# Adaptive-LayerNorm attention and MLP block with gradients on one Trainium2 core: dO stores by ScalarE, two modulation gradients in the W2 gradient's loop, and another row order in the end stage

## The chip, the cores and the metric

The kernel runs on one core of a Trainium2 chip. The metric is the device time of one execution in microseconds (us); smaller is better. The core's engines have separate instruction streams: TensorE (PE: matmuls and, in a queue of its own, weight loads), VectorE (DVE), ScalarE (ACT), GpSimd (POOL) and SyncE (SP, which here only issues DMAs). DMAs are issued by SP, POOL and, after the change, by ACT. PSUM is the memory that PE writes to; SBUF holds the working tiles.

## What is computed

A block with attention and an MLP, both with LayerNorm and modulation from a condition `c`, forward and backward. With S = 2048 rows, D = 512, 32 heads of 16, F = 1792:

```python
mod = (_silu(c) @ w_mod).reshape(c.shape[0], 6, 1, -1)
sa, ca, ga, sb, cb, gb = (mod[:, 0].copy(), ...)
h = _layernorm(x, axis=-1) * (1 + ca) + sa
x = x + ga * _A_ref(h, A_wqkv, A_wo)
h = _layernorm(x, axis=-1) * (1 + cb) + sb
x = x + gb * _B_ref(h, B_w1, B_b1, B_w2, B_b2)
```

`_A_ref` is softmax attention of 32 heads, then times wo; `_B_ref` is relu(h @ w1 + b1) squared, times w2, plus b2. Beside the block's output (out_0) the kernel returns the gradients of x (out_1), wqkv (out_2), wo (out_3), w1, b1, w2, b2 (out_4 to out_7), c (out_8) and w_mod (out_9), for a given gradient `grad_out` of the output. The gradient of w_mod has six parts of 512 columns, one for each of sa, ca, ga, sb, cb, gb (j = 0 to 5). Part j is the outer product of silu(c) with the summed gradient of that modulation vector; the same sums, multiplied with w_mod, give out_8.

## The kernel before, in words

Rows are cut into 16 tiles of 128 (ST = 16), the rows into four chunks of 512 (SC = 4), D into four blocks of 128 (DT), F into 14 (FT), the heads into eight quads of four (NQ). The run has four stages.

*Forward attention* (about 0 to 985 us): the exponentials of the scores on ACT (L389), the rest on the other engines. While it runs, the MLP and its backward of the chunks that are done run in the background (`gen_mlp`, L1135); it produces dx1, the gradient at the input of the second half, row tile by row tile.

*The middle*, `last_chunk` (about 985 to 1169 us): the last chunk's MLP and its backward, then the weight gradients. `gen_dw1` (L955 to L1015) walks over the 14 blocks of F; each block is 64 matmuls of 128 x 128 into a PSUM tile `dps` (L988, three buffers), one small f32 matmul with a diagonal matrix (L993), four ACT scalings (L1001), and on DVE per block of D a scaling to the output tile dw1 (L1002, two buffers) and two products summed into `dcb_part` and `dsb_part` (L1004, L1007); then POOL stores dw1 to out_4. `gen_dw2` (L1017 to L1061) does the same for w2: 16 matmuls of 128 x 512 a block, two DVE products, an out_6 store on POOL. For both, the first 12 row tiles of the transposed activations come from DRAM through DMA transposes on SP (`turned`: tile tm_blk, four buffers, L941) and the last four row tiles from SBUF (tm_l, one transpose for four blocks, L945, from tile auT for dw1). `turn_do` (L872 to L881) transposes the attention output's gradient dO on PE, copies it by ACT into dOTq and, for every second row tile, stores it to DRAM (L881, on SP). `open_bwd` sets up the tiles of the backward, among them mask tiles `m` that DVE clears (L1344). At its end `last_chunk` issues on SP the loads that the backward starts with, one piece for every eight steps of `gen_dw2`: the operands of the first pair of heads, of the first quad, and WmT, the transposed and modulated wqkv (`load_wmt`, four pieces of 384 KB).

*Backward attention*, `attn_bwd` (about 1166 to 2433 us): for each of eight quads, two pairs of heads; PE, ACT and DVE are each about 98% busy. The gradients ds of the scores are transposed partly by DMA (dsT<-ds, SP). Loads for the next pair are issued by POOL one piece at a time, each behind a small copy (`tick`, L1511) that waits for a point of DVE's work. Pair (7,0) so loads eight pieces.

*The end*, `phase6` (2433 to 2562.6 us): the gradient of wqkv (`dw`, L1572), dx row tile by row tile (`dx`, 12 matmuls of L1664 each, then ACT and DVE, out_1 stores on POOL), the gradient of wo (`dwo`, four blocks of 16 matmuls, L1707, over all 16 row tiles of dx1 in bf16, tile dx1b), and the six parts of the modulation gradient (`mod`: one f32 matmul L1728, an ACT copy L1730, four ACT scalings L1733, one store L1734, four DVE dots L1592). The tile dx1b is cast by ACT (L1702) from the f32 rows of dx1 that `dx` loads (`load_a`, two row tiles at once with three DMA transposes and two loads on SP). `dx` works on a row in place, so the cast stands ahead of ACT's step L1678 on the same tile; the rows 12 to 15 have casts of their own ahead of `dwo(0)`.

Order: PE and SP follow the order in which the program issues everywhere, POOL also from the backward on, and every engine in the end stage, whose order is written out by hand (L1737 to L1813). In the middle the order on DVE, ACT and POOL is the scheduler's. Each engine runs its instructions in order, so an instruction that waits holds all behind it on that engine.

Of the kernel before, what the change touches and what calls it, by code (L numbers as in the profile page):

```python
# [10 lines left out]
F32 = mybir.dt.float32  # L11
# [94 lines left out]
class K:  # L106
# [29 lines left out]
    def build(self, ctx: ExitStack):  # L136
        tc, nc = self.tc, self.nc
        self.dram_pool = ctx.enter_context(tc.tile_pool(name="dram", bufs=1, space=DRAM))
        self.pp = ctx.enter_context(tc.tile_pool(name="persist", bufs=1))
        S, D, F, H, NQ, ST, DT, FT = self.S, self.D, self.F, self.H, self.NQ, self.ST, self.DT, self.FT  # L140
        self.xhat1_d = self.dram("xhat1_d", [S, D], BF16)
        self.qtm_d = self.dram("qtm_d", [NQ, P, ST * 4 * DH], BF16)
        self.ktm_d = self.dram("ktm_d", [NQ, P, ST * 4 * DH], BF16)
        self.QTq_d = self.dram("QTq_d", [NQ, P, S], BF16)
        self.KTq_d = self.dram("KTq_d", [NQ, P, S], BF16)
        self.VTq_d = self.dram("VTq_d", [NQ, P, S], BF16)
        self.dOTq_d = self.dram("dOTq_d", [NQ, P, S], BF16)
        self.O_d = self.dram("O_d", [S, D], BF16)
        self.O32_d = self.dram("O32_d", [S, D], F32)
        self.xhat2_d = self.dram("xhat2_d", [S, D], BF16)  # L150
        self.aT_d = self.dram("aT_d", [FT, P, S], BF16)
        self.duT_d = self.dram("duT_d", [FT, P, S], BF16)
        self.dx1_d = self.dram("dx1_d", [S, D], F32)
        self.vaug_d = self.dram("vaug_d", [P, ST * H * (DH + 1)], BF16)
        self.dOp_d = self.dram("dOp_d", [NQ, P, ST * 4 * DH], BF16)
        self.dqkv_d = self.dram("dqkv_d", [S, 3 * D], BF16)
        self.WmT_d = self.dram("WmT_d", [DT, P, 3 * DT * P], BF16)
        self.open_pools = {}
        self.phase0()
        with tc.manual_schedule(engines={mybir.EngineType.PE, mybir.EngineType.SP}):  # L160
            self.phase_fwd()
            with tc.manual_schedule(engines={mybir.EngineType.PE, mybir.EngineType.SP, mybir.EngineType.Pool}):
                self.phase5()
            with tc.manual_schedule(engines=ALL):
                self.phase6()
        for name in list(self.open_pools)[::-1]:
            self.close_pool(name)
# [98 lines left out]
    def phase_fwd(self):  # L266
# [14 lines left out]
        self.kvs = pp.tile([P, 1], F32, name="kvs")  # L281
        pp.tile([P, 112], BF16, name="pad")
# [474 lines left out]
    def last_chunk(self, bg, O_b, x0s, o32):  # L757
# [116 lines left out]
        def turn_do(k):  # L874
# [4 lines left out]
            if k % 2:  # L879
                t0 = (st0 + k - 1) * P  # L880
                nc.sync.dma_start(self.dOTq_d.rearrange("g p s -> p g s")[:, :, t0:t0 + 2 * P], self.dOTq[:])  # L881
# [44 lines left out]
        pieces = self.pair_pieces(0, 0) + pieces + self.load_wmt()  # L926
# [25 lines left out]
    def gen_dw1(self, sb, xh2, duT):  # L952
# [14 lines left out]
        def load(ft):  # L967
            r = turned(sb, duT, self.duT_d, ft)
# [5 lines left out]
            blks.append((r, w, diag))  # L974

        for ft in range(2):
            load(ft)
        yield 0
        for ft in range(FT):
            if ft + 2 < FT:  # L980
                load(ft + 2)
            else:
                yield ("dw1", 0)
            du, w1_blk, diag = blks[ft]
# [32 lines left out]
    def gen_dw2(self, sb, g_tm, aT, tb):  # L1017
        nc, io = self.nc, self.io
        D, ST, FT = self.D, self.ST, self.FT
# [11 lines left out]

        load(0)
# [3 lines left out]
        for ft in range(FT):  # L1036
# [12 lines left out]
            nc.gpsimd.tensor_tensor(dgb[:], dgb[:], tmp[:], ALU.add)  # L1049
            if ft == FT // 2:  # L1050
# [84 lines left out]
    def gen_mlp(self, sc, O_b):  # L1135
# [63 lines left out]
        for k in range(4):  # L1199
# [11 lines left out]
            nc.vector.tensor_copy(dxb[:], dx1[:])  # L1211
            dxT = mk.tile([P, DT, P], BF16, name="dxT", bufs=2)
# [89 lines left out]
    def phase5(self):  # L1302
# [10 lines left out]
        nc.gpsimd.memset(self.dc_part[:], 0.0)  # L1313
# [34 lines left out]
    def load_wmt(self):  # L1348
# [3 lines left out]
        return [(self.WmT[:, kt].rearrange("p n k -> p (n k)"), self.WmT_d[kt]) for kt in range(DT)]  # L1352
# [37 lines left out]
    def attn_bwd(self):  # L1390
# [97 lines left out]
        for g in range(NQ):  # L1488
            for jp in range(2):
                if jp == 0:  # L1490
                    if g + 1 < NQ:
                        Tn, later = self.load_group(g + 1)
                    else:
                        Tn, later = None, self.wq_pieces(1)
# [103 lines left out]
    def phase6(self):  # L1598
# [44 lines left out]

        def load_a(i):
            s2 = 2 * i
# [12 lines left out]
        def dx(st):  # L1658
            dqT, dx1s = nxt[st // 2]
            k = st % 2  # L1660
# [15 lines left out]
            if st < 12:  # L1676
                cast(st)
# [5 lines left out]
            (nc.sync if st == ST - 1 else nc.gpsimd).dma_start(out1_v[:, st, :], o[:])  # L1683
            if k and st // 2 + 3 < ST // 2:
                load_a(st // 2 + 3)
# [14 lines left out]

        def cast(st):
            nc.scalar.copy(dx1b[:, st, :], nxt[st // 2][1][st % 2][:])  # L1702
# [23 lines left out]
        def mod(j):  # L1726
# [4 lines left out]
            o = sb.tile([P, DT, D], BF16, name="dwm7")  # L1731
            for kt in range(DT):
                nc.scalar.activation(o[:, kt, :], dm[:], ACT.Copy, scale=self.scT[:, kt:kt + 1])  # L1733
            nc.gpsimd.dma_start(dwm_v[:, :, j * D:(j + 1) * D], o[:])  # L1734
# [3 lines left out]
        for j in (5, 3):  # L1738
            load_wmod(j)
        dgs[5] = self.dgb_acc  # L1740
        diag(3, self.dsb_col)
        diag(4, self.dcb_col)
# [8 lines left out]
        dx1b = sb.tile([P, ST, D], BF16, name="dx1b")  # L1751
        O_tm = sb.tile([P, ST, D], BF16, name="O_tm")
# [3 lines left out]
        mod(3)  # L1756
        dx(1)
        load_wmod(4)
        dw(2, 2, dpp, "dp")
        dx(2)  # L1760
        load_wmod(0)
        dw(2, 3, dpp, "dp")
        mod(4)
# [4 lines left out]
        load_wmod(1)  # L1768
# [23 lines left out]
        for st in range(12, ST):  # L1792
            cast(st)
        dwo(0)
        dx(12)
# [90 lines left out]
```

## Time and profile before

| what | value |
|---|---|
| time of four runs | 2564.32, 2573.64, 2564.89, 2577.24 us |
| median | 2569.27 us |
| the profiled execution's own time, and its span | 2564.32 us, 2562.6 us |
| busy in the span: PE, ACT, DVE, POOL | 96%, 90%, 69%, 21% |
| middle, 1075.00 to 1080.00: PE busy | 0.43 of 5.00 us |
| end stage: mean of an ACT cast to dx1b (L1702), and of a scaling for out_9 (L1733) | 608 ns, 711 ns |

The profile is of one execution. Its times are us from the start of the span; a group's row gives the operation with its output and input tiles, the number of instructions, busy time and mean; what stands in brackets behind a row of a timeline is how long the engine had stood idle before it, and whose work ended that idle time. Busy shares are means over stages with different limits: what a change in a stage is worth is read from that stage.

### The profile page before, as it was taken

The numbers are of one execution on the slowest core, as the hardware profiler recorded it, in microseconds if no ns is written. First come the engines' busy times: TensorE is split into PE (matmuls) and PEld (weight loads), VectorE is DVE, ScalarE is ACT, GpSimd is POOL, SyncE is SP. The second block draws the span as 40 slices with busy tenths as digits, with TensorE's granted clock in tenths as the row PEclk, the third lists the DMA queues.
The fourth block names the chain that finished last, engine by engine and source line by source line (L and its number), as shares of the span: only waits on it lengthen the run. The fifth ranks groups of instructions, "written<-read, shape, count | busy, mean of one in ns | idle before, by whom it ended". The sixth has DMA issues, their size and how long they took to land.

```text
span 2562.6 us, 77543 instructions
## 1 busy us (share of the span) xinstructions
PE 2466.9 (96%) x31011; PEld 1225.7 (48%) x31239; DVE 1763.3 (69%) x3651; ACT 2315.4 (90%) x3761; POOL 550.6 (21%) x1098
## 2 busy tenths in 40 slices
PE   8999899999999999999999999999999999999997
PEld 4555555555555554763444444444444444444443
DVE  6222223323322344768999999999999999999876
ACT  7999999999999996417999999999999999999854
POOL 3454521320221121352111111111111111101122
PEclk9999999999999999999999999999999999999998
DMA  4588652440351154799999999999999999999985
GB/s 165 118 183 193 172 95 85 100 112 22 113 127 49 39 135 113 159 208 227 199 199 201 201 200 201 199 204 203 198 203 198 201 204 202 201 198 207 219 218 152
DMA packets 1192481, 424.33 MB, mean 166 GB/s; under 512 B 1137572, under 2 KB 1161254, under 8 KB 1192118
## 3 DMA queue, kind: packets, MB, share of 16 engines
q1 hardware_dynamic: 1156198, 321.87, 65.0%
q0 software_dynamic: 35920, 97.49, 12.7%
q8 instruction: 244, 4.00, 0.7%
q14 instruction: 119, 0.97, 0.1%
HBM read 73.21 MB, written 61.87 MB: 53 GB/s over the span
## 4 chain that ended last, share of the span: by engine, by line
PE 61%; ACT 30%; issue 5%; DMA 3%; DVE 1%; POOL 1%; ACTq 0%; DVEq 0%; POOLq 0%
ACT pu L389 26%; PE st L1523 19%; PE acckv L1416 10%; PE accq L1438 8%; PE st L386 4%; PE dp L1462 2%; ACT pu L1527 2%; PE st L1481 2%; PE dps L1042 2%; PE accbank L320 2%; PE dp L1572 2%; DMA dsT<-ds 1%; PE dps L988 1%; PE st L1664 1%; PE pps L1204 1%
## 5 line engine op out<-in xcount | busy, mean ns | idle before, releaser
L1464 DVE TENSOR_TENSOR ds<-dp,pu 128x512 bf16<-128x512 f32 x2048 | 1236.1, 679 | 13.2 <-PE dp L1462 10.8
L1527 ACT ACTIVATE pu<-st 128x512 bf16<-128x512 f32 x2048 | 1073.9, 612 | 75.5 <-PE st L1523 50.3
L389 ACT ACTIVATE pu<-st 128x1024 bf16<-128x1024 f32 x992 | 912.1, 1077 | 4.9 <-PE st L386 4.3
L386 PE MATMUL st<-QTm,KTq 128*128 128x512 bf16 x1859 | 561.4, 377 | 26.9 <-ACT pu L389 6.0
L320 PEld LDWEIGHTS <-pu 128*128 128x128 bf16 x8192 | 347.3, 96 | 236.1 <-issue 3.1
L320 PE MATMUL accbank<-Vaug,pu 128*128 128x17 bf16 x8192 | 357.6, 171 | 8.3 <-ACT Vaug L520 1.1
L1462 PE MATMUL dp<-m,q 64*128 64x512 bf16 x1024 | 344.4, 381 | 1.1 <-DVE g2w L1048 0.7
L1462 PE MATMUL dp<-m,dOTg 64*128 64x512 bf16 x1024 | 344.0, 381 | 0.0
L1438 PEld LDWEIGHTS <-dsT 128*128 128x128 bf16 x8192 | 239.8, 96 | 214.0 <-issue 208.8
L1523 PE MATMUL st<-m,QTg 64*128 64x512 bf16 x1024 | 319.1, 381 | 9.7 <-ACT pu L1527 8.1
L1523 PE MATMUL st<-m,q 64*128 64x512 bf16 x1024 | 318.8, 381 | 9.5 <-ACT pu L1527 7.3
L386 PEld LDWEIGHTS <-KTq 128*128 128x128 bf16 x1984 | 188.4, 96 | 177.0 <-issue 125.6
L1511 POOL COPY tick<-ds 1x1 bf16<-1x1 bf16 x215 | 37.9, 176 | 1016.2 <-DVE ds L1464 1016.2
L1416 PE MATMUL acckv<-pu,q 128*16 128x512 bf16 x1024 | 154.0, 381 | 0.0
L1416 PE MATMUL acckv<-ds,Qg 128*16 128x512 bf16 x1024 | 154.0, 381 | 0.0
L1416 PE MATMUL acckv<-ds,q 128*16 128x512 bf16 x1024 | 154.0, 381 | 0.0
L1416 PE MATMUL acckv<-pu,dOg 128*16 128x512 bf16 x1024 | 154.0, 381 | 0.0
L1482 ACT COPY dsT<-st 128x512 bf16<-128x512 bf16 x256 | 152.5, 596 | 0.9 <-PE dp L1462 0.4
L1438 PE MATMUL accq<-Kg,dsT 128*128 128x16 bf16 x4096 | 143.5, 170 | 4.2 <-DMA dsT<-ds 4.0
L1438 PE MATMUL accq<-q,dsT 128*128 128x16 bf16 x4096 | 144.0, 170 | 0.4 <-DMA dsT<-ds 0.3
L300 POOL DMA_DIRECT2D QTm<-QTq_d x124 | 63.5, 514 | 341.9 <-PE st L386 320.8
L327 DVE RECIPROCAL rl<-accbank 128x4 f32<-128x4 f32 x128 | 22.9, 179 | 165.2 <-PE accbank L320 164.9
(368 smaller groups left out, 2813.5 us busy)
## 6 DMA issues: line engine op xcount, KB each, us to landing
KTq<-KTq_d POOLq DMA_DIRECT2D x24, 512.0 KB, 4.0
duT_d<-auT POOLq DMA_DIRECT2D x3, 1792.0 KB, 7.7
aT_d<-rT POOLq DMA_DIRECT2D x3, 1792.0 KB, 11.1
KTq_d<-KTq SPq DMA_DIRECT2D x32, 128.0 KB, 1.9
QTq_d<-ev_fm SPq DMA_DIRECT2D x32, 128.0 KB, 3.3
VTq_d<-vT POOLq DMA_DIRECT2D x4, 1024.0 KB, 6.6
dsT<-ds SPq DMA_TRANSPOSE x256, 6.9
dx<-dx_d SPq DMA_DIRECT2D x16, 256.0 KB, 4.0
```

The costliest lines, as they stand in the source:

```text
L300: nc.gpsimd.dma_start(QTm[j][32 * j:32 * j + 32, :], self.QTq_d[g, 32 * j:32 * j + 32, 512 * qc:512 * (qc + 1)])
L320: nc.tensor.matmul(acc[:, a, sub, :], lhsT=pu[:, a, sub * P:(sub + 1) * P], rhs=Vaug[:, kb, h, :], start=(kb == 0 and a == 0 and sub == 0) ...
L386: nc.tensor.matmul(stt[:, a, :], lhsT=KT[:, kb * P:(kb + 1) * P], rhs=QTm[2 * jp + a][:], start=True, stop=True)
L389: nc.scalar.activation(pu[:], stt[:], ACT.Exp, scale=self.scale)
L1042: nc.tensor.matmul(pt[:], lhsT=a[st], rhs=g_tm[:, st, :], start=(st == 0), stop=(st == ST - 1))
L1416: nc.tensor.matmul(acckv[r:r + DH, :], lhsT=T[n][:, ib, col:col + DH], rhs=src[:, a, :], start=(ib == 0), stop=(ib == ST - 1))
L1438: nc.tensor.matmul(accq[:, ib, a, :], lhsT=dsT[:, (i * 2 + a) * 4 + sub, :], rhs=T["K"][:, 4 * c + sub, col:col + DH], start=(c == 0 and i ...
L1462: nc.tensor.matmul(dp[:], lhsT=T["dOT"][rd, ib * P:(ib + 1) * P], rhs=masked["VT"][2 * jp + a][rd, 512 * c:512 * (c + 1)], start=True, sto ...
L1464: nc.vector.tensor_tensor(dsg[:, i, a], dp[:], pu[:, a, :], ALU.mult)
L1482: nc.scalar.copy(dsT[:, 0:4, :], tp[:])
L1523: nc.tensor.matmul(stt[:], lhsT=T["QT"][rs, q], rhs=masked["KT"][2 * jp + a][rs, c0:c0 + 512], start=True, stop=True)
L1527: nc.scalar.activation(pu[:, a, :], stt[:], ACT.Exp, scale=self.scale)
```

## The change

1. *dO stores.* In the last chunk ACT issues the two stores of dOTq to DRAM (L881), right after its copies; SP did.
2. *Blocks three ahead.* `gen_dw1` requests its transposed blocks (tm_blk, tm_l) three blocks ahead, the w1 blocks and diagonals two ahead as they were.
3. *Two modulation gradients* (j = 3, 4: sb and cb) leave the end stage for `gen_dw2`. The diagonal matrices, the w_mod load and eight stores of out_9 (one for each block of D) go with them. Matrices and products lie in the tiles O32 and auT, which are free by then. `dc_part` is cleared at the start of the program.
4. *WmT* is loaded by POOL in eight pieces (196 KB each) in pair (7,0) of the backward, in place of four pieces by SP at the end of the middle.
5. *End stage.* Rows are walked in the order 0 to 7, 12 to 15, 8 to 11. The bf16 rows 8 to 11 of dx1b are written to DRAM (dx1b_d) in the forward, while chunk SC - 2 is worked on, and loaded by one DMA of POOL; the other 12 are cast by ACT inside `dx`, and the four separate casts ahead of `dwo(0)` are gone. The thirteenth dx stands ahead of `dwo(0)`, not behind it. The tile of the out_9 parts (dwm7) is one per block of D with five buffers and a store each, where one tile of four blocks had one buffer and one store. w_mod parts are loaded in the order 5, 0, 1, 2.

```diff
@@ turn_do, last_chunk
-                nc.sync.dma_start(self.dOTq_d.rearrange("g p s -> p g s")[:, :, t0:t0 + 2 * P], self.dOTq[:])
+                nc.scalar.dma_start(self.dOTq_d.rearrange("g p s -> p g s")[:, :, t0:t0 + 2 * P], self.dOTq[:])
...
-        pieces = self.pair_pieces(0, 0) + pieces + self.load_wmt()
+        pieces = self.pair_pieces(0, 0) + pieces
@@ gen_dw1
+        dus = [turned(sb, duT, self.duT_d, ft) for ft in range(3)]
         for ft in range(2):
             load(ft)
         yield 0
         for ft in range(FT):
+            if ft + 3 < FT:
+                dus.append(turned(sb, duT, self.duT_d, ft + 3))
             if ft + 2 < FT:
                 load(ft + 2)
@@ gen_dw2
+        mods = {2: (3, self.dsb_col), 5: (4, self.dcb_col)}
...
+            if ft in mods:
+                j, col = mods[ft]
+                if ft == min(mods):
+                    low = self.ra.tile([P, FT * 512], BF16, name="auT")
+                    hi = self.ra.tile([P, 4, D], F32, name="O32")
+                    nw = DT * D
...
+                nc.gpsimd.dma_start(wm, io["w_mod"].rearrange("(kt p) n -> p kt n", p=P)[:, :, j * D:(j + 1) * D])
+                for kt in range(DT):
+                    nc.scalar.activation(dg[:, kt * P:(kt + 1) * P], self.ident_f[:], ACT.Copy, scale=col[:, kt:kt + 1])
+            if ft - 2 in mods:
+                pt = self.dps.tile([P, 512], F32, name="dps")
+                nc.tensor.matmul(pt[:], lhsT=self.ones_f[:], rhs=dg, start=True, stop=True)
+                yield 2
+                nc.scalar.copy(dm, pt[:])
+                for kt in range(DT):
+                    c = 2 * nw + kt * D
+                    o = low[:, c:c + D]
+                    nc.scalar.activation(o, dm, ACT.Copy, scale=self.scT[:, kt:kt + 1])
+                    nc.gpsimd.dma_start(io["out_9"][kt * P:(kt + 1) * P, j * D:(j + 1) * D], o)
+                    c = 2 * nw + DT * D
+                    nc.vector.scalar_tensor_tensor(low[:, c:c + D], dm, 1.0, wm[:, kt], ALU.mult, ALU.mult,
+                                                   accum_out=self.dc_part[:, kt, j:j + 1])
@@ gen_mlp
+            if sc == SC - 2:
+                nc.gpsimd.dma_start(self.dx1b_d.rearrange("(st p) d -> p st d", p=P)[:, k, :], dxb[:])
@@ load_wmt
-        return [(self.WmT[:, kt].rearrange("p n k -> p (n k)"), self.WmT_d[kt]) for kt in range(DT)]
+        return [(self.WmT[:, kt, n:n + 6].rearrange("p n k -> p (n k)"), self.WmT_d[kt, :, n * P:(n + 6) * P])
+                for kt in range(DT) for n in range(0, 3 * DT, 6)]
@@ attn_bwd
-                        Tn, later = None, self.wq_pieces(1)
+                        Tn, later = None, self.wq_pieces(1) + self.load_wmt()
@@ phase6
+        order = [*range(ST - 8), *range(ST - 4, ST), *range(ST - 8, ST - 4)]
...
-            if st < 12:
-                cast(st)
+            if n < ST - 4:
+                nc.scalar.copy(dx1b[:, st, :], gp[:])
...
-            o = sb.tile([P, DT, D], BF16, name="dwm7")
             for kt in range(DT):
-                nc.scalar.activation(o[:, kt, :], dm[:], ACT.Copy, scale=self.scT[:, kt:kt + 1])
-            nc.gpsimd.dma_start(dwm_v[:, :, j * D:(j + 1) * D], o[:])
+                o = sb.tile([P, D], BF16, name="dwm7", bufs=5)
+                nc.scalar.activation(o[:], dm[:], ACT.Copy, scale=self.scT[:, kt:kt + 1])
+                nc.gpsimd.dma_start(dwm_v[:, kt, j * D:(j + 1) * D], o[:])
...
-        for j in (5, 3):
+        for j in (5, 0):
             load_wmod(j)
         dgs[5] = self.dgb_acc
-        diag(3, self.dsb_col)
-        diag(4, self.dcb_col)
...
+        nc.gpsimd.dma_start(dx1b[:, ST - 8:ST - 4, :], tm_v(self.dx1b_d))
...
-        mod(3)
         dx(1)
-        load_wmod(4)
+        load_wmod(1)
...
-        load_wmod(0)
         dw(2, 3, dpp, "dp")
-        mod(4)
         dx(3)
...
-        load_wmod(1)
...
         dx(11)
-        for st in range(12, ST):
-            cast(st)
+        dx(12)
         dwo(0)
-        dx(12)
```

## The prediction, made before the changed kernel ran

> **What bounds the kernel now.** I read the engines' busy shares first, then the chain of work that ended last, then the stretches of the two stages that the change touches. TensorE (PE) is busy for 2466.9 of 2562.6 us, and the chain says the same of the path:
>
> ```profile
> PE 2466.9 (96%) x31011; PEld 1225.7 (48%) x31239; DVE 1763.3 (69%) x3651; ACT 2315.4 (90%) x3761; POOL 550.6 (21%) x1098
> PE 61%; ACT 30%; issue 5%; DMA 3%; DVE 1%; POOL 1%; ACTq 0%; DVEq 0%; POOLq 0%
> ```
>
> ACT's 30% are the exponentials of forward attention (L389), which the change doesn't touch. So I look only for time in which PE stands still, or runs slowly, in the middle (about 990 to 1169 us) and in the end stage (2433 to 2562.6). The middle's busy time by stretches (columns: window, its length, busy PE, PEld, DVE, ACT, POOL, granted clock, DMA share, GB/s) and PE's timeline:
>
> ```profile
> 1070.00:1075.00 5.00, 5.00 (x91) 4.99 (x88) 3.50 (x15) 1.80 (x6) 2.44 (x4) 1.00 1.39 212
> 1075.00:1080.00 5.00, 0.43 (x5) 0.26 (x3) 3.48 (x14) 0.00 (x0) 1.19 (x2) 0.93 1.05 200
> 1080.00:1085.00 5.00, 4.80 (x46) 4.80 (x46) 3.99 (x18) 1.80 (x6) 0.75 (x1) 0.50 0.59 130
> ```
> ```profile
> 1080.19 1.44 PE L988 MATMUL dps<-tm_blk,xh 128*128 128x128 bf16 x12 [4.76 <-DVE junk L1004]
> ```
>
> PE stands 4.76 us for a PSUM buffer of dps that VectorE (DVE) must free, and then works at clock 0.50 and 0.89: the 64 matmuls of that block take 6.55 us instead of 3.57, so 3 us more, and 0.46 us of waiting follows at 1091.3. In all 8.2 us. Why DVE was late stands in its timeline:
>
> ```profile
> 1068.89 0.91 DVE L1344 MEMSET m<- 128x1024 uint32 x1 [2.22 <-DMA dOTq_d<-dOTq]
> ...
> 1076.19 0.35 DVE L1002 SCALAR_TENSOR_TENSOR dw<-dps,opcbT,t 128x128 bf16<-128x128 f32 x1 [2.38 <-DMA out_dram<-dw]
> ```
>
> The memset of a mask tile waits until the second dO store has landed; behind it stand the steps of dw1, whose store then goes out late (1070.52) and makes the block two later wait. The store of dO is SP's:
>
> ```profile
> 1050.62 0.37 SPq L881 DMA_DIRECT2D dOTq_d<-dOTq  x1
> 1051.04 7.15 SPq L941 DMA_TRANSPOSE tm_blk<-duT_d  x3
> ...
> 1062.90 0.37 SPq L881 DMA_DIRECT2D dOTq_d<-dOTq  x1
> ```
>
> In the end stage PE is continuous from 2433.65 to 2507.6 and is held before and within the first block of dwo (L1707), by ACT:
>
> ```profile
> 2518.25 2.32 PE L1707 MATMUL gps<-dx1b,O_tm 128*128 128x512 bf16 x9
> 2523.89 0.59 PE L1707 MATMUL gps<-dx1b,O_tm 128*128 128x512 bf16 x1 [3.32 <-ACT dx1b L1702]
> 2526.14 0.58 PE L1707 MATMUL gps<-dx1b,O_tm 128*128 128x512 bf16 x1 [1.66 <-ACT dx1b L1702]
> 2528.01 2.14 PE L1707 MATMUL gps<-dx1b,O_tm 128*128 128x512 bf16 x4 [1.28 <-DMA out_dram<-dx]
> ```
> ```profile
> 2520.20 2.56 ACT L1733 ACTIVATE dwm<-dm,scT 128x512 bf16<-128x512 f32 x4 [2.26 <-DMA out_dram<-dwm]
> ...
> 2527.35 2.16 ACT L1702 CAST dx1b<-dx 128x512 bf16<-128x512 f32 x4
> ```
>
> ACT waits 2.26 us for the store of the one dwm buffer; the casts of rows 10 and 11 come late after it, and four more (rows 12 to 15) follow. PE's last four matmuls of the block and the 12 of dx(12) then take 2.14 and 4.26 us, where a later four take 1.03 and a later 12 take 2.59: slow clock after the gap.
>
> [...]clock 0.50 after the 4.76 us gap, back within 6.6 us; after 3.32 + 1.66 us, a block at half speed. [...] The trace of before has no store from ACT here; it shows that the second store, issued after SP's run of transposes, needed 5.99 us (1062.90 to 1068.89).
>
> **The change, part by part**, against the profiled execution (2564.32 us: span 2562.6 and 1.7 around it, 4.95 under the median of 2569.27; I take the difference over to the median).
>
> *End stage, dwo.* From 2518.25 to the end of dwo(3) at 2547.35 PE needs 29.10 us. Its work there is 64 dwo matmuls (16 take 3.45 in the chain: 13.80) and two dx of 12 (2.59 each: 5.18), 18.98 in all. In the new order dx(12) goes ahead of dwo(0), rows 8 to 11 of dx1b come by DMA from a copy made in the forward, dwm has five buffers so that the 2.26 us wait goes, and the four casts of 2.16 us go (12 of 16 casts stay, each with its dx). Moving ACT's steps forward by 2.26, the cast of the last row wanted ends at about 2524.05; PE does dx(12) from 2518.25 to 2520.84 and reaches the last matmul of dwo(0) near 2524.1. What is late next is this cast, by 0.1 to 0.5. So 29.10 - 18.98 - 0.1 = **-10.0 us**. The transposes for dx(12), which SP issues up to 2511.9 and which need 5.1 to 5.8 us to land, and the 0.5 MB load on POOL far ahead, are covered by 2518.25.
>
> *End stage, two modulation gradients less.* Each is a f32 matmul of 0.86 us on PE, in a stretch where PE never stops: **-1.72**. Their ACT work (8 diagonals, 2.5 us; twice 0.57 + 4 x 0.64), 8 DVE dots of 0.77 (6.2), two loads and two stores on POOL ran beside PE: 0.
>
> *The same two in the middle.* PE is continuous from 1086 to 1166 as well: **+1.72**. DVE's 6.2 us: it is busy 8.6 to 8.9 of 10 us in dw1 but, by its blocks, about 13 of 25 us in dw2: 0. ACT is at 4.7 of 10: 0. POOL gets two loads (0.76 each) and eight stores (0.54), at 5.5 of 10: 0 by time. By order not: the first load goes into the old auT and waits until the last tm_l, issued by SP at 1096.59 with a landing of 3.7 to 7.9, has read it (1100.3 to 1104.5). Behind it on POOL stand the dw1 stores of blocks 8 and on and later w1 loads; DVE waits for those stores, PE for DVE. The slack of dps at blocks 11 to 13 is 2.1 us, then 1.1 to 2.9 in dw2. Bounds 0 to +2.5; I take **+0.8**.
>
> *dO stores on ACT, blocks three ahead.* SP loses two issues, ACT gains two (0.37 each, PE doesn't wait for ACT here). ACT's copy for the second store ends at 1062.87 and SP issued at 1062.90: no earlier issue. The transposes of blocks 2 and 3 leave at about 1027, where the DMA share is 0.91 falling to 0.26, and not at 1051; tm_blk has four buffers, so "three ahead" takes SP no further than the buffers did. So the store may land earlier by 0 to 2.5 us (4.1 to 4.5 is the median landing of such stores). Against it: DVE's order moves. The first memset stands three operations sooner, two stand ahead of block 2's last step (its store goes out 1.7 us later after the landing), and six, not five, ahead of block 3's last (+0.91). One fewer is left behind it, so the 0.46 wait goes. The 4.76 us stall becomes 3.3 to 6.3: bounds -8.2 (also the clock loss goes) to +1.5; I take **-0.5**.
>
> *WmT in eight pieces on POOL during pair (7,0), not by SP at 1162.* PE waits 1.0 us for dsT in 1260 to 2420, and a pair with 16 pieces on POOL (2340 to 2420) has PE busy 78.70 of 80 against 78.80 with eight. 0; if the 1.57 MB held the dsT transposes back for their own length at 200 GB/s, +7.9. At the handover PE waits 1.0 us: 0 to -1.0. *Forward*: four 128 KB stores more on POOL and a memset at the start, neither near PE's waits: 0 (0 to +0.5).
>
> Sum: -10.0 - 1.72 + 1.72 + 0.8 - 0.5 = **-9.7 us**: 2554.6 for the profiled execution, 2559.6 on the median.
>
> **The rivals.**
> A, *the stall in the middle goes too* (0.25): with the early transposes the dO store lands in 4 us[...]. For it: DMA share 1.10 to 1.39 at 1060 to 1075, by traffic that moves away. Against: DVE's new order. A further -7.7: 2551.9.
> B, *the end gains only part* (0.17): dx(12) or the last casts are late for another reason (transposes land after 2518, ACT still behind with mod(1)). Then only the wait of 2.26 and 1.72 go, with +2 in the middle: 2567.3. Against it: the transposes have 6 us.
> C, *POOL held by the w_mod load* (0.08): if tm_l lands much later than 7.9 us, the dw1 stores stop, dw has two buffers, DVE stops two blocks later (7.7 us of PE time), PE after dps's slack of 2.1. Up to a hold of about 10 us nothing much is lost; each us more costs one[...]. It decides from a hold of about 20 us, where the loss passes 10 and eats the end's gain. At 25 us: 15 + 3 - 11.7 + 1.7, so +8: 2577. Against it: no landing over 7.9 for tm_l.
> That the stores' move does nothing (the change not doing what it says there) is inside my forecast.
>
> **How the numbers follow.** Forecast 0.50 (its own range 2554 to 2564), A 0.25, B 0.17, C 0.08. The range 2549 to 2570 takes in A and B with 1 in 10 left out at either end. A measurement of this kernel can tell 0.5%, 12.8 us: under 2556.4 is faster. Faster: 0.22 of A, 0.10 of the forecast: 0.32. Slower, over 2582: 0.04, of C and of what I didn't see. Same: 0.64.
>
> **What would show it.** Right: dwo(0) to dwo(3) with dx(12), dx(13) in about 19.1 us of PE with no wait over 0.5; mods at about 1115 to 1145 with no new PE wait; a wait for junk L1004's successor near 1075 of 3.3 to 6.3 us, with clock 0.50 after it. A is right if that clock stays 1.00; B if PE still waits over 2 us for ACT or dqT near 2518 to 2528; C if PE waits for dps at 1100 to 1125. Wrong altogether if pair (7,0) shows PE waits for dsT over 1 us, or the end has a wait elsewhere (the dg wait of 1.03 at 2507.6 growing).

## The result and the profile after

The changed kernel takes 2560.35 us (median of 37 runs, 2555.39 to 2570.23), the kernel before 2566.20 in the runs beside it (58 runs, 2561.02 to 2588.31). The ratio is 0.9972, with a 95% interval of 0.9961 to 0.9982: about 7.2 us less, where 9.7 had been forecast. The medians differ by 5.85 us. The gain is clear of noise, but smaller than the 12.8 us at which the forecast would have called the kernel faster. The profiled execution took 2560.64 us, its span is 2558.8; it is 3.7 us shorter than the profiled one of before. From the page of the changed kernel, the busy time of each engine and the chain's shares by engine:

```profile
PE 2465.3 (96%) x31011; PEld 1223.4 (48%) x31239; DVE 1766.6 (69%) x3651; ACT 2314.8 (90%) x3757; POOL 567.9 (22%) x1137
PE 60%; ACT 30%; issue 5%; DMA 3%; DVE 1%; POOL 1%; DVEq 0%; ACTq 0%; POOLq 0%
```

PE is as full as before, so a comparison of stages has to tell it. I cut each execution at four marks that both traces have: the small f32 matmul that closes the first block of dw1 (block 0), the first score matmul of the backward, the first matmul `dp<-dk_t` at its end, and the end of the span.

| stage | before | after | difference |
|---|---|---|---|
| start to the small matmul of dw1's block 0 | 1055.36 | 1055.29 | -0.07 |
| middle, from there to the backward | 110.96 | 117.54 | +6.58 |
| backward | 1259.83 | 1262.91 | +3.08 |
| end | 136.45 | 123.06 | -13.39 |

So the end stage gave more than was forecast for it (11.7), and the middle took more than was forecast for it (2.0). The middle first. Its 6.58 us have three parts: the first ten blocks of dw1, with the stall at 1075, take 42.82 us for 43.39 (-0.57); from there to the first matmul of the W2 gradient on tm_l it takes 23.70 us for 18.27 (+5.43, all of it new loss); the rest is longer by the two matmuls of the modulation gradients (+1.72). PE's timeline after the change, around 1080 (start, duration, operation, idle time before it and who ended it), and the stretches of the middle (columns as in the prediction):

```profile
1080.81 1.44 PE L992 MATMUL dps<-tm_blk,xh 128*128 128x128 bf16 x12 [4.48 <-DVE junk L1008]
```

```profile
1075.00:1080.00 5.00, 1.33 (x21) 1.16 (x19) 3.07 (x15) 0.43 (x2) 0.77 (x3) 1.00 1.25 200
1080.00:1085.00 5.00, 4.20 (x51) 4.19 (x51) 4.64 (x21) 1.80 (x6) 1.16 (x2) 0.66 0.20 62
...
1110.00:1122.00 12.00, 8.41 (x79) 5.53 (x79) 8.54 (x56) 3.60 (x12) 3.60 (x5) 0.86 1.12 190
```

Before the change the last of these stretches was:

```profile
1110.00:1122.00 12.00, 11.95 (x112) 7.85 (x111) 9.99 (x59) 3.60 (x12) 3.79 (x6) 1.00 1.06 204
```

The stall at 1075 is still there: 0.80, 4.48 and 0.65 us of waits and a block of 4.93 us in place of 3.57, 7.29 us against 8.20 before. The waits themselves are longer than before (5.93 us for 5.22). What is shorter is the slow clock: by the record of the granted clock that each trace has, it lasted 3.41 us here (1080.30 to 1083.71) and 6.83 us before (1079.31 to 1086.14). The memset still waits for the dO store, which takes as long when ACT issues it (issued 1062.83, landed 1068.56: 5.73 us) as when SP did (5.99). DVE's timeline after the change:

```profile
1068.56 0.91 DVE L1375 MEMSET m<- 128x1024 uint32 x1 [2.80 <-DMA dOTq_d<-dOTq]
...
1108.34 0.35 DVE L1006 SCALAR_TENSOR_TENSOR dw<-dps,opcbT,t 128x128 bf16<-128x128 f32 x1 [2.56 <-DMA out_dram<-dw]
...
1114.52 0.35 DVE L1006 SCALAR_TENSOR_TENSOR dw<-dps,opcbT,t 128x128 bf16<-128x128 f32 x1 [2.87 <-DMA out_dram<-dw]
```

The last two are new: blocks 10 and 11 of dw1 wait for the stores of blocks 8 and 9. POOL's timeline shows why, and PE's what it cost:

```profile
1102.65 0.76 POOL L1064 DMA_DIRECT2D auT<-in_w_mod_dram  x1 [3.10 <-DMA tm_l<-auT]
1103.40 0.76 POOL L1014 DMA_DIRECT2D out_dram<-dw  x1
...
1105.31 0.80 POOL L1064 DMA_DIRECT2D auT<-in_w_mod_dram  x1
1106.10 0.76 POOL L1014 DMA_DIRECT2D out_dram<-dw  x1
```

```profile
1111.36 0.83 PE L992 MATMUL dps<-tm_blk,xh 128*128 128x128 bf16 x12 [1.27 <-DVE junk L1008]
...
1117.54 0.38 PE L1047 MATMUL dps<-g_tm,tm_blk 128*128 128x512 bf16 x1 [2.16 <-DVE junk L1008]
1118.07 3.90 PE L1047 MATMUL dps<-g_tm,tm_blk 128*128 128x512 bf16 x10 [0.16 <-issue]
```

And the same matmuls of the W2 gradient in the kernel before, then the stretch of those ten matmuls after the change, with a granted clock of 0.59:

```profile
1114.43 2.75 PE L1042 MATMUL dps<-g_tm,tm_blk 128*128 128x512 bf16 x11
```

```profile
1118.07:1121.97 3.90, 3.90 (x11) 1.50 (x11) 3.56 (x24) 1.64 (x6) 0.71 (x1) 0.59 1.17 230
```

The scheduler put both w_mod loads between the dw1 stores. The first waits 3.10 us for the last tm_l. The store behind it goes out at 1103.40 and block 10 may start only at 1108.34; the store of block 9 follows at 1106.10, right behind a second load of 512 KB, and block 11 starts at 1114.52, 8.4 us later (the median landing of these stores was 4.1 before). PE waits 3.43 us in two parts. Ten matmuls then take 3.90 us at a mean granted clock of 0.59, where eleven took 2.75 in the kernel before (a few records of matmuls are missing in a trace, here one of the block's twelve in either; from the first of them to the first on tm_l it is 4.27 us for 2.59).

In the end stage the chain of the changed kernel, in pieces (start, duration, engine and line) goes through dx and dwo without a gap:

```profile
2519.70 7.77 PE st L1699 x36
...
2527.53 6.89 PE gps L1739 x31
2534.42 2.59 PE st L1699 x12
...
2543.92 2.60 PE st L1699 x12
```

36 matmuls of dx(10), dx(11) and dx(12) are followed at once by dwo(0). From the start of dx(12), 2527.53 - 2.59 = 2524.94, to the end of dwo(3) at 2543.92 it is 18.98 us, where it was 29.10. That makes -10.1 of the stage's 13.39 us. Another 1.7 us lie at its very start, up to the column sums (10.78 us for 12.46), where PE waits for the last dsT, before and after:

```profile
2431.64 0.92 PE L1438 MATMUL accq<-Kg,dsT 128*128 128x16 bf16 x28 [3.29 <-DMA dsT<-ds]
```

```profile
2440.57 0.86 PE L1470 MATMUL accq<-Kg,dsT 128*128 128x16 bf16 x28 [2.62 <-DMA dsT<-ds]
```

This part isn't the change's: over all traces it takes 8.3 to 14.9 us.

### The profile page after: what moved, and what is told of

It is laid out like the page before. It is cut to its first block, busy times and chain, and to the rows that moved or that the text cites. A ratio compares the mean times of both kernels' runs of the same rounds, so it can differ in the third digit from the quotient of the medians.

```text
span 2558.8 us, 77624 instructions
## 1 busy us (share of the span) xinstructions
PE 2465.3 (96%) x31011; PEld 1223.4 (48%) x31239; DVE 1766.6 (69%) x3651; ACT 2314.8 (90%) x3757; POOL 567.9 (22%) x1137
## 4 chain that ended last, share of the span: by engine, by line
PE 60%; ACT 30%; issue 5%; DMA 3%; DVE 1%; POOL 1%; DVEq 0%; ACTq 0%; POOLq 0%
ACT pu L391 26%; PE st L1555 19%; PE acckv L1448 10%; PE accq L1470 8%; PE st L388 4%; PE dp L1494 3%; ACT pu L1559 2%; PE st L1513 2%; PE dps L1047 2%; DMA dsT<-ds 2%; PE accbank L322 2%; PE dp L1604 1%; PE st L1699 1%; PE pps L1234 1%; PE dps L992 1%
## 5 line engine op out<-in xcount | busy, mean ns | idle before, releaser
L1496 DVE TENSOR_TENSOR ds<-dp,pu 128x512 bf16<-128x512 f32 x2048 | 1236.4, 679 | 15.8 <-PE dp L1494 12.8
```

The source lines that it names most:

```text
L1496: nc.vector.tensor_tensor(dsg[:, i, a], dp[:], pu[:, a, :], ALU.mult)
```

## The experiments

All are edits of the changed kernel, or put parts of it on the kernel before; each is compared with runs of the kernel before on the same chip. The stages are cut as above; they are of one profiled execution each, and that isn't always a typical one: those of e1, f1 and i4 were the longest of their kernel, that of g1 lay 13.7 us above its median.

| run | ratio to before, interval | middle | backward | end | PE's waits for dqT |
|---|---|---|---|---|---|
| after | 0.9972, 0.9961 to 0.9982 | 117.54 | 1262.91 | 123.06 | 0 |
| e1_mods_in_end | 0.9954, 0.9935 to 0.9972 | 111.68 | 1263.23 | 135.05 | 0 |
| e3_wmt_by_sp | 0.9975, 0.9962 to 0.9989 | 118.24 | 1261.40 | 122.60 | 0 |
| f1_wmod_by_sp | 0.9958, 0.9941 to 0.9975 | 113.22 | 1261.30 | 131.11 | 6.7 |
| f2_masks_by_act | 0.9927, 0.9907 to 0.9947 | 106.68 | 1263.14 | 122.27 | 0 |
| g1_masks_wmod_wmt | 0.9919, 0.9895 to 0.9944 | 104.60 | 1262.01 | 139.42 | 13.5 |
| h1_end_stage_alone | 0.9991, 0.9969 to 1.0014 | 110.79 | 1264.52 | 142.17 | 13.2 |
| h2_one_dwm_buffer | 0.9981, 0.9964 to 0.9998 | 115.50 | 1263.09 | 135.73 | 8.0 |
| h3_stores_sp_two_ahead | 0.9948, 0.9934 to 0.9963 | 117.11 | 1262.14 | 128.20 | 3.9 |
| i4_masks_wmod | 0.9897, 0.9861 to 0.9933 | 104.33 | 1259.53 | 135.12 | 8.1 |
| k2_end_alone_no_O | 0.9974, 0.9959 to 0.9989 | 109.82 | 1263.75 | 130.33 | 0 |
| h4_row_order_as_before | 0.9973, 0.9957 to 0.9989 | 119.30 | 1262.98 | 128.35 | 0 |
| k4_masks_mods_in_end | 0.9899, 0.9865 to 0.9932 | 102.61 | 1262.21 | 123.34 | 0 |

The runs e1 to f2 shared one chip, g1 to h3 a second one, i4 to k4 a third, so ratios of different groups are compared with care. How much one stage differs between executions shows in the middle of the five kernels that have the two w_mod loads on POOL and the memsets on DVE (after, e3, h2, h3, h4): 115.50 to 119.30 us.

**e1_mods_in_end**: the block in `gen_dw2` goes, the calls in the end stage come back.

```diff
-            if ft in mods:
-                ...
+        diag(3, self.dsb_col)
+        diag(4, self.dcb_col)
...
+        mod(3)
         dx(1)
+        load_wmod(4)
...
+        mod(4)
         dx(3)
```

> The changed kernel with the two modulation gradients (j = 3, 4) back in the end stage; all else as changed. Theory (the w_mod load on POOL, with the dw1 stores behind it, cost the middle 5.1 us beyond the 1.72 us of PE work): the PE waits of 1.27 and 2.16 us at 1110 to 1118 and the slow clock after them are gone, the backward starts at about 1166.0 in place of 1172.8, the end stage is 1.7 to 2 us longer, so 4.5 to 5 us less in all (about 2555.5 on the median of 2560.4). Rival (the dO stores and DVE's order of memsets cause the late waits): the backward still starts after 1170 and the time is the same within 1.5 us.

The backward starts at 1165.72, as the theory says, and the two late waits are gone: the middle is 5.86 us shorter. The rival's cause, DVE's order, is ruled out for the late waits. The time is 0.9954 of before; its interval overlaps that of the changed kernel, so the gain is shown in the trace and not in the time. (The profiled execution was the longest of this kernel, with ACT 5.55 us behind an out_9 store in the end stage.)

**e3_wmt_by_sp**: WmT by SP at the end of the middle, four pieces.

```diff
-                        Tn, later = None, self.wq_pieces(1) + self.load_wmt()
+                        Tn, later = None, self.wq_pieces(1)
...
-        pieces = self.pair_pieces(0, 0) + pieces
+        pieces = self.pair_pieces(0, 0) + pieces + self.load_wmt()
```

> The changed kernel with WmT loaded by SP in four pieces at the end of the middle, as before. Theory (WmT's pieces on POOL push the dsT transposes back in pair (7,0)): the PE waits for dsT of 1.30 and 0.81 us at 2329 and 2340 are gone and the backward, from its first matmul to the first dp<-dk_t, takes about 2 us less than 1262.9; the time falls by 1 to 2 us. Rival (the longer backward is what differs from one execution to the next anyway): 1262 to 1264, with waits for dsT of 2 us or more elsewhere, and the time the same within 1 us.

The two waits in pair (7,0) are gone, as the theory says, but the time isn't shorter: the ratio is that of the changed kernel. In their place PE waits at the start of the backward, for ACT's copy to dsT. First the changed kernel's longer wait in pair (7,0), then this one:

```profile
2329.51 0.46 PE L1470 MATMUL accq<-Kg,dsT 128*128 128x16 bf16 x12 [1.30 <-DMA dsT<-ds]
```

```profile
1178.21 0.58 PE L1554 MATMUL st<-m,q 64*128 64x512 bf16 x1 [1.59 <-ACT dsT L1513]
```

All traces together say the same. With WmT on POOL, five of nine have a wait of 1.30 to 1.75 us for dsT at this place of pair (7,0); with WmT on SP, none of five. With WmT on SP all five wait 0.30 to 2.25 us for ACT's copy at the start; with WmT on POOL, none of nine. So WmT's place seems to move a wait, from the start of the backward to pair (7,0). Over all traces the backward takes 1259.5 to 1263.2 us with WmT on POOL (nine executions, mean 1262.3) and 1259.8 to 1264.5 with WmT on SP (five, mean 1262.3): the 3.08 us of the first table are what one execution differs from another. In the middle this execution had the stall of 1075 at 7.56 us, because the store of block 2 landed later still (DVE waited 4.69); its late waits were 0.83. Which store lands late varies; a wait of PE of 4.3 us or more near 1080 stands in all ten traces with the memsets on DVE.

**f1_wmod_by_sp**: one word.

```diff
-                nc.gpsimd.dma_start(wm, io["w_mod"]...
+                nc.sync.dma_start(wm, io["w_mod"]...
```

> The changed kernel with the two w_mod loads of the W2 gradient's loop issued by SP, between its transposes, in place of POOL. Theory (POOL's order: the load waits for auT with the dw1 stores behind it, and its 0.5 MB go ahead of theirs): the waits of 1.27 and 2.16 us are gone, the backward starts at about 1168.0, 4.8 us less. Rival (the 1 MB and eight stores more are the load, whoever issues them): PE still waits 3 us or more between 1108 and 1160, and the time is the same within 1.5 us.

The backward starts at 1168.39, 4.4 us earlier; PE has no wait for dps after 1092. The same bytes, issued between SP's transposes, cost nothing there:

```profile
1123.91 0.95 SPq L1064 DMA_DIRECT2D auT<-in_w_mod_dram  x1
```

So it was not the traffic as such. The edit changes two things, though: the engine that issues, and the time, as SP gets to the loads about 20 and 30 us later than POOL did. Whether POOL's wait of 3.10 us, the bytes that POOL issues ahead of the stores, or the traffic at just that time cost most isn't separated.

**f2_masks_by_act**: ACT writes the zeros of the mask tiles, from dcb_col times 0, so that they can't be scheduled before dw1 is done.

```diff
-        for ms in self.masked.values():
-            for m in ms:
-                nc.vector.memset(m, 0.0)
...
         fill.until("half")
+        for ms in self.masked.values():
+            for m in ms:
+                nc.scalar.activation(m, self.dcb_col[:, 0:1].to_broadcast([P, self.S]), ACT.Copy, scale=0.0)
```

> The changed kernel with the eight mask tiles cleared by ACT once dcb_col is there (at about 1120), in place of DVE's memsets, which wait for the dO store. Theory (the memset that waits for the dO store, and the memsets, make DVE late and so PE): the waits of 0.80, 4.48 and 0.65 us and the slow block near 1072 to 1091 are gone, the backward starts at about 1165.5, 7.3 us less, if ACT's 15 us of clearing fit beside the W2 gradient. Rival (dw1 has two buffers and its stores need 5 us to land, so DVE is held by them without any memset): PE still waits over 2 us for dps between 1065 and 1095, and the gain is under 3 us.

All waits before 1095 are gone, and one of 2.20 us is left at 1113.6 with no slow clock after it (12 matmuls in 2.75 us). The middle is 10.9 us shorter than in the changed kernel, more than the 7.3 expected: 7.8 us come from the first ten blocks of dw1, and the rest because the loss by the late stores fell from 5.4 to 2.4 us. That DVE, 7.3 us of memsets lighter (8 x 0.91), meets those stores with more slack is a likely reason, not a shown one. The edit takes from DVE both the wait for the store and the memsets' own time; which of the two counts more isn't separated. ACT's clearing took 14.6 us (12.68 for seven tiles and 1.91) beside the W2 gradient. The waits of PE between 1040 and 1165, in all:

```profile
PE dps L1050 <- DVE junk L1011: 2.2, 1, 2.2
PE dp L1494 <- DVE g2w L1056: 0.7, 1, 0.7
PE dp L1494 <- DVE ds L1496: 0.3, 1, 0.3
```

**g1_masks_wmod_wmt**: f1, f2 and e3 together.

> The changed kernel with all three moves: masks cleared by ACT, w_mod loads of the W2 gradient by SP, WmT by SP at the end of the middle. Theory (three separate costs): the backward starts at about 1158.0, that is 2.2 us before the 1160.3 of the version with the masks alone, its last wait for dps (2.20) being gone, and the backward is 1 to 2 us shorter: about 2544.5 on the median, against 2548.0. Rival (the middle is then bound by something else, DMA or POOL, and SP's queue before the backward by WmT): no gain over 2548.0.

The middle is as expected: the backward starts at 1158.27 and no wait for dps is left. The time doesn't decide: the medians are 2547.82 and 2548.02 us, but from two chips, on which the kernel before differs by 5 us (2569.15 and 2564.09), and the intervals of the two ratios (0.9919 and 0.9927) overlap. The profiled execution took 2561.5 us and lost 13.5 us in the end stage, to which nothing had been done. PE's timeline there:

```profile
2515.43 7.33 PE L1698 MATMUL st<-WmT,dqT 128*128 128x512 bf16 x24 [9.44 <-DMA dqT<-dq_t]
```

SP's, in the same execution: one transpose sat 12.04 us in SP's queue, where the median of these eight was 2.75.

```profile
2491.92 12.04 SPq L1681 DMA_TRANSPOSE dqT<-dv_t  x1
```

**h1_end_stage_alone**: the kernel before with part 5 of the change only (w_mod parts loaded in the order of before).

> The kernel before with the end stage of the change alone (row order, rows 8 to 11 of dx1b by DMA with their stores in the forward, dwm in five buffers, dx(12) ahead of dwo(0)); the modulation gradients, the dO stores, the blocks and WmT as before. Theory (the prediction's step): dwo(0) to dwo(3) with dx(12) and dx(13) take 19 to 20 us of PE in place of 29.1, the time falls by 9 to 10.5 us. Rival (with the two modulation gradients still in the end stage ACT is late anyway, and the gain needs both): 3 to 6 us.

Neither: 0.9991, its runs spread from 2557.49 to 2578.18. There is no wait for ACT's casts, and the first dwo matmul to the last take 16.6 us, as in the changed kernel (16.4; 29.1 before, with dx(12) among them). So the part does what was meant, but ahead of it PE waits 13.2 us for dqT (9.8 at once):

```profile
PE st L1670 <- DMA dqT<-dq_t: 13.2, 3, 9.8
```

```profile
2450.00:2530.00 80.00, 67.36 (x298) 29.18 (x297) 54.70 (x143) 39.87 (x81) 27.57 (x47) 0.94 1.15 213
```

The second fence is the stretch 2450 to 2530 of the same trace: DMA share 1.15.

**k2_end_alone_no_O**: h1, and the 2 MB of O_tm left out.

```diff
-            nc.gpsimd.dma_start(O_tm[:, b, :], tm_v(self.O_d)[:, b, :])
+            nc.gpsimd.memset(O_tm[:, b, :], 0.0)
```

> The end stage of the change alone on the kernel before, as in the earlier run with a ratio of 0.9991, but with the four loads of O_tm (2 MB) in the end stage left out: POOL clears the tile, so out_3 and what is made of it are zero. Theory (the DMA engines are full in the end stage, and the dqT transposes come late because of it): the waits for dqT fall from 13 us to under 3, ratio 0.993 to 0.996. Rival (ACT is late with six modulation gradients in the end stage, or the chip was just slow): dqT waits as before or waits for ACT of 5 us or more, ratio over 0.998.

The waits for dqT are gone, the DMA share of the stretch is 0.88, and PE is busy for 78.97 of 80 us:

```profile
2450.00:2530.00 80.00, 78.97 (x405) 35.30 (x398) 61.11 (x159) 48.55 (x97) 33.42 (x51) 1.00 0.88 225
```

The median is 2562.91 us (before on this chip 2569.01), where h1 had 2571.72 (before 2569.15). The ratio, 0.9974, is less good than the theory's 0.993 to 0.996, and its interval overlaps that of h1. So the crowded DMA engines as the cause of the waits are supported by one trace on each side, no more: two kernels with the same end stage, g1 and the changed one, show 13.5 and 0 us. How much of the time these waits take on average isn't settled. A rival that wasn't tried alone is the change's own load of 0.5 MB into dx1b: the two traces without it (before, h4) have no wait for dqT, six of the twelve with it have one.

**h2_one_dwm_buffer**: one tile and one store for a part again.

```diff
             for kt in range(DT):
-                o = sb.tile([P, D], BF16, name="dwm7", bufs=5)
-                nc.scalar.activation(o[:], dm[:], ACT.Copy, scale=self.scT[:, kt:kt + 1])
-                nc.gpsimd.dma_start(dwm_v[:, kt, j * D:(j + 1) * D], o[:])
+                nc.scalar.activation(o[:, kt, :], dm[:], ACT.Copy, scale=self.scT[:, kt:kt + 1])
+            nc.gpsimd.dma_start(dwm_v[:, :, j * D:(j + 1) * D], o[:])
```

> The changed kernel with one dwm tile of four blocks and one store again. Theory (the 2.26 us wait for the store is the first cause of the late casts): ACT waits 2 to 3 us before the second part, PE 1.5 to 4 us near the end of dwo(0)[...], so 2 to 6 us more. Rival (dx(12) ahead of dwo(0) hides it): less than 1 us more.

ACT waits 6.42 us for the store (0.16 in the changed kernel), but PE only 0.2 for ACT, as it had just waited 6.43 for dqT. The ratio is 0.9981. The wait on ACT is as the theory says; whether it reaches PE when dqT is on time stays open.

**h3_stores_sp_two_ahead**: `nc.sync` in place of `nc.scalar` for the dO stores, and `turned` back in `load`, two blocks ahead.

> The changed kernel with the dO stores issued by SP and the blocks two ahead again. Theory (these parts don't set the stall at 1075 to 1086, DVE's memset behind the store and the memsets do, and the store's data are ready at the same time): the backward starts within 1.5 us of 1172.8, the waits before 1095 keep a sum of 5 to 7 us, the time is the same within 1.5 us. Rival[...]: the backward starts 2 us or more later.

The middle takes 117.11 us, 0.4 less than with these parts, with waits of 5.01 and 3.40 us: the theory holds, parts 1 and 2 don't shorten the middle. All traces bear it out. Where nothing is lost (f2, g1, i4, k4) the first ten blocks of dw1 take 35.04 us; with the old stores and two blocks ahead (before, h1, k2, h3) they take 42.25 to 43.39, with the new ones (after, e1, e3, f1, h2, h4) 42.82 to 47.81. The ratio, 0.9948, is better than that of the changed kernel, 6 us for which these blocks are too little; the two were not timed on one chip, and I leave it open.

**h4_row_order_as_before**: rows 0 to 15, four casts, dx(12) behind dwo(0), no bf16 rows through DRAM; dwm keeps its five buffers.

```diff
-        order = [*range(ST - 8), *range(ST - 4, ST), *range(ST - 8, ST - 4)]
+        order = [*range(ST)]
...
-        dx(12)
+        for st in range(12, ST):
+            nc.scalar.copy(dx1b[:, st, :], nxt[st // 2][1][st % 2][:])
         dwo(0)
+        dx(12)
```

> The changed kernel with rows 0 to 15 in order, four separate casts ahead of dwo(0), dx(12) behind it, and no bf16 copy through DRAM; dwm stays at five buffers. Theory (the order and the casts carry most of the 10 us, the buffers 2 to 3): PE waits 3 to 5 us for dx1b casts in dwo(0), with slow clock after it, 5 to 8 us more than the changed kernel, ratio to before 0.999 to 1.001. Rival (the end stage is bound by its DMAs, so the order hardly matters, and 0.5 MB less is loaded): within 2 us of the changed kernel, ratio 0.996 to 0.998.

In the trace the theory holds: PE waits 1.02, 2.00 and 1.28 us for casts, four matmuls then take 2.15 us, and the end stage is 5.3 us longer than after. Its dwo matmuls take 26.5 us from the first to the last, where before they took 29.1 and in the twelve traces with the new order 16.4 to 17.8, without dx(12)'s 2.6. So the order and the casts carry most of the step, the five buffers about 2.6. The ratio, 0.9973, is in the rival's range. Both can be true if in the runs that don't wait for casts dqT is late at the same place; that isn't shown.

**i4_masks_wmod**: f1 and f2 together.

> The changed kernel with the masks cleared by ACT and the two w_mod loads by SP; WmT by POOL as changed. Theory (memsets on DVE and the w_mod load on POOL are the whole loss of the middle): no wait for dps, backward starts at 1158.3 within 0.3, no wait for dsT copies at its start; ratio to before 0.990 to 0.993. Rival (the end stage is bound by its DMAs and takes back what comes earlier): ratio 0.994 or more, with waits for dqT that grow by what the middle gave.

**k4_masks_mods_in_end**: e1 and f2 together.

> The changed kernel with the masks cleared by ACT and the two modulation gradients back in the end stage. Theory (their move takes 2 MB of DMA and 1.72 us of PE out of a crowded end stage and costs the middle about 4 us by POOL's order): the backward starts at about 1156.5, dqT waits in the end stage are larger than with the gradients moved, and the time is 0 to 4 us over that of the version with masks by ACT and w_mod by SP. Rival (moving them never pays): 2 us or more below that version.

i4 starts its backward at 1158.25, without any wait for dps: the memsets and the place of the w_mod loads were the whole avoidable loss of the middle, 117.54 - 104.33 = 13.2 us (the two matmuls stay). k4 starts it at 1157.75; its middle is 102.61 us, 1.72 less than that of i4, just the two matmuls of 0.86. In the time the two can't be told apart: the ratios are 0.9897 and 0.9899, each with an interval of 9 us to either side, and k4's median is 2.15 us the higher one. So whether moving the two gradients pays, once their loads don't stand on POOL, stays open. That they relieve the end stage's DMA isn't shown: the profiled execution of k4 had no wait for dqT, that of i4, the longest of six, 8.1 us. Both beat the kernel before and the changed one; i4's median is 2544.23 us, beside 2569.01 before.

## Why the prediction was right, and where its steps were off

The likeliest case was right in direction and in its main step; the measured gain is about 7.2 us for 9.7 forecast. That the sum came so near is in part luck. In the two traces the middle lost 4.6 us more than forecast and the backward 3.1, the end stage gave 1.7 more, and the medians differ by more than these two executions. And the forecast of 2559.6 us lies so close to 2560.35 because it started from a median of four runs, 2569.27, where 58 runs give 2566.20.

- *dwo*: -10.0 forecast; 29.10 became 18.98 in the trace, -10.1. Right, and not by chance: the step is as short in every trace with the new order. What was late next, the last cast, didn't show. As time of the whole kernel it isn't shown alone: h1 has the short step and a ratio of 0.9991, h4 the longer one and that of the changed kernel.
- *Two gradients out of the end, into the middle*: -1.72 and +1.72. In the middle i4 against k4 gives 1.72. In the end stage, from the column sums (2438.61 before, 2446.52 after) to the start of dx(12), it is 79.64 against 78.42 us, 1.2 less, in one execution each.
- *dO stores and blocks*: -0.5 forecast, 8.20 became 7.29, -0.9. The number is luck. Right is that the memset and the store stayed in each other's way and that the clock fell to 0.50; only f2 removed that. But the waits grew by 0.71 us, the 0.46 us wait that I said would go became 0.65, and the gain is a slow clock of 3.41 us in place of 6.83. In f1 and h4, which have this part too, that block takes 6.30 and 6.22 us, where it took 6.39 before and 4.93 in the changed kernel. Over all traces the part gains nothing.
- *w_mod load on POOL*: +0.8 forecast, bounds 0 to 2.5. This term was mis-sized: f1 shows 4.3 us (117.54 - 113.22), and in the five traces with the load on POOL and the memsets on DVE the loss is 1.0 to 6.0 us (5.4 in the changed kernel), in f2 2.4, in f1 and e1 none. The wait that I had priced, POOL's hold until tm_l has landed, was 3.10 us and within the 1100.3 to 1104.5 that I gave for it. What I left out is that POOL then issues 1 MB ahead of the second store, and that this store takes 8.4 us, twice the median of 4.1; that it takes so long because of these bytes is likely, not shown alone. The new PE waits at 1100 to 1125 are the sign that I had set for rival C. Its mechanism came true, at about 4 us and without the long hold that I asked for.
- *WmT*: 0 forecast, and the mean of 1262.3 us either way supports it; the 3.08 us in the first table are differences between executions. The sign that I had set for "wrong altogether", a wait over 1 us for dsT in pair (7,0), did come (1.30 us). It was a bad sign: the wait is real, and a like one at the start of the backward went, where I had put 0 to -1.0.
- *dqT*: I wrote that the transposes are covered. In the changed kernel's trace they are; in six of the twelve experiments PE waited 3.9 to 13.5 us for them, which is near what rival B named. This is a cost that the word "covered" left out. Between 2450 and 2530 the six executions with such waits had a DMA share of 1.07 to 1.15, the others 0.88 to 1.14, so the share alone doesn't tell them apart. The waits are likely a part of why the runs give less than the trace of dwo does; how large, these runs don't settle.

When a wait is followed by the slow clock, the traces show only in part. In before, after, f1, h4 and k2 a wait of 4.30 to 4.76 us between 1075 and 1086 was followed by slow matmuls each time: 4.93 to 6.39 us for the 64 of a block that takes 3.57 otherwise. But so was the 2.16 us wait in the changed kernel, 4.0 us after another (granted clock 0.50 from 1117.84 to 1121.26), while the 2.20 us wait in f2 (1111.39 to 1113.59) was not: the 12 matmuls behind it took 2.75 us, as 12 had taken ahead of it. In the clock records of before and after the slow spells begin a whole number of steps of 3.413 us apart: at 318.14, 1079.31, 2430.99, 2523.15 and 2557.28 before, at 319.12, 1080.30, 1117.84, 2442.22 and 2554.86 after (from 1080.30 to 1117.84 it is 11 steps). Each lasts one, two or three whole steps, but for the last, at the kernel's end. So a shorter gap alone would not have made rival A's sign, a clock that stays at 1.00, certain; how much standing still is enough, these traces don't settle.

## What to carry to other kernels

Before a load is put into a loop, look at where the scheduler will place it, which stores will stand behind it on the issuing engine, and how many buffers those stores hold. Price the bytes ahead of the stores as well as the wait: here the wait was 3.10 us, and the second store, behind 1 MB, took 8.4 us where the median was 4.1 (that the bytes did it is likely, not shown). Where an operation waits for a store only because it reuses its memory, give it to an engine that isn't feeding the critical one, or tie it to data that come later, rather than make the store faster: here doing both made the middle 10.9 us shorter (f2), while a store by ACT took 5.73 us for SP's 5.99. And where a stage's DMA share is about 1 (0.88 to 1.15 between 2450 and 2530 in these traces), treat a transfer that lands in time in one trace as a cover that may fail in the next.

## What wasn't expected of the hardware

The issue of one DMA transpose of dqT took between 1.23 and 13.02 us of SP's queue in the end stage. The longest was 4.0 us in the kernel before and 4.5 in k2 (DMA share between 2450 and 2530: 1.03 and 0.88), but 12.04 in g1 (1.15) and 13.02 in f1 (1.12).

In the changed kernel a store from POOL that follows two 512 KB loads from the same engine took 8.4 us, where 4.1 was the median before. It doesn't always: in the same order the slowest dw1 store between 1100 and 1120 took 5.5 us in e3 and 5.8 in h2, but 10.3 in h3 and 10.9 in h4.

And of two waits of 2.2 us one was followed by a granted clock of 0.50 (the changed kernel, 1115.37 to 1117.54), and the other by matmuls at full pace (f2, 12 in 2.75 us). In before and after the slow spells begin a whole number of steps of 3.413 us apart.
